# Induced set attention with a leaky feed-forward: the maxima of the first attention by one full-size product, and a shorter pipeline for its first batch

## The chip, the cores and the metric

The kernel runs on one core of a Trainium2 chip. The metric is device time in microseconds (us) from one launch. Engines are named as in the profile: PE is TensorE (matmuls), PEld its weight loads, DVE VectorE, ACT ScalarE, POOL GpSimd, SP the engine that issues most DMAs.

## The reference

Four batches of 12480 tokens with 128 channels pass an induced set attention (32 inducing points), and then a feed-forward with a leaky ReLU.

```python
def mab(q, kv):
    s = scale * (q @ kv.transpose(0, 2, 1))
    s = s - s.max(-1, keepdims=True)
    a = np.exp(s)
    a /= a.sum(-1, keepdims=True) + 1e-09
    return a @ kv
h = mab(I, x)            # first attention: I is [4, 32, 128], x is [4, 12480, 128]
attn = mab(x, h)         # second attention: every token against the 32 rows of h
hid = attn.reshape(49920, 128) @ w_in        # w_in is [128, 2048]
out = np.maximum(0.01 * hid, hid) @ w_out    # w_out is [2048, 128]
```

## The kernel before

A batch is cut into six groups of 2048 tokens and a rest of 192 tokens (`RG`, handled first), so a batch has seven groups. The scores of a group in the first attention stand as a 128 x 512 tile: partition (j, m) holds inducing point m against the j-th quarter of the group's tokens. Softmax over all tokens of a batch needs one maximum per m, kept as a running maximum over the groups. `running(b, g, sp)` (line 273) does this for one group. It is a generator: each `yield` is a place where the caller may put other work. In the kernel before its steps are

- L281, DVE: copy the scores out of PSUM and take each partition's maximum, `rm` [128, 1];
- L292, PE: `mx_ps`, a product of `rm` (as weights, one column) with the 128 x 128 identity. It turns the 128 maxima into one row on one partition;
- L295 and L301, DVE: reduce that row over j to 32 maxima, multiply by -SCALE and repeat four times, `mrow` [1, 128];
- L306, PE: `mb_ps`, a product of `mrow` (as weights, one partition) with a single one. It turns the row back into a column over the 128 partitions;
- L314 or L316, DVE: the running (negated) maximum `nm`;
- L321 and L325, ACT: `al`, the factor for what earlier groups gave, and the exponentials `e` with their sums `zg`; L334, DVE: the running sum `zs`.

Later the exponentials are transposed (L418, `ay`), multiplied with x on PE (`h_ps`, L393, in `accumulate`) and added up on DVE (`hacc`, L408). From the sum comes h (`normalise`: `hs` L458, `hT_ps` L461), which the second attention and the feed-forward of that batch need.

All work is issued in an order written out by hand, and each engine works through its own queue in that order. There are two stages.

The first batch has no other work to hide behind. `first_batch` (line 467) runs rounds: round i transposes group i on PE (`xT_ps`, L501) and copies it on ACT (L504), computes its scores (`s_ps`, L269), and moves earlier groups on by some steps of their generators. Three groups are under way at a time: `accumulate` is called for group i - 3. After each part of a round, steps of background lanes are issued, by the tables `ROUNDS` and `DRAIN`. The lane `l` turns the float64 weights into float32: per quarter of a matrix one ACT operation, six on DVE (L119, L123, L127, L132, L137, L141), two on POOL (L144 and L145), and for w_out a split into high and low parts (ACT L200, POOL L201). The lane `t` transposes w_in (`winT_ps`, L214) and `m` multiplies the weights (`w_ps`, L226, four parts).

After that the feed-forward runs 1568 units, each one product of the first layer (`ph`, L770) and three of the second (`po`, L798), three units ahead: ACT makes `ghi` (L778) and DVE `glo` (L780). Between units, steps of the later batches' first attention (`first_scores`, `first_values`), of the second attention, and of what is left of the weights are issued. 21 of the 28 groups pass `running` here. `yield HEAVY` delays the next steps by three units.

Of the kernel before, what the change touches and what calls it, by code (L numbers as in the profile page):

```python
# [9 lines left out]
F32 = mybir.dt.float32  # L10
# [9 lines left out]
def induced_attention_then_leaky_ffn(  # L20
# [8 lines left out]
    """Induced set attention, then a leaky-relu feed-forward, on 4 x 12480 tokens.  # L29

    The second attention gives x2 = a @ h with a [tokens, 32], so x2 @ w_in = a @ (h @ w_in): the
    first product contracts over 32 only.  Operands are split exactly into float32r parts
    (hi + lo = float32); the four part products of the first product are stacked along the
    contraction, (a_hi, a_hi, a_lo, a_lo) against (W_hi, W_lo, W_hi, W_lo).  With
    g = max(0.01 h, h) = 0.99 relu(h) + 0.01 h, the linear part is a @ (h @ w_in @ w_out).
    The first attention runs over groups of tokens with a running maximum.

    A group holds J tiles of 32 * K tokens: token K * (32 j + r) + k is column (k, r) of tile j,
    so that 32 x 32 transposes lead between [(j, r), (k, m)] and [(j, m), (k, r)].
    """  # L40
    nc = tc.nc
# [23 lines left out]
    # what a long instruction of VectorE weighs in slots of the feed-forward; no lane goes on  # L65
    # before it is paid off
    HEAVY = 3
    # loads of w_in: after which loads of x of the first batch
    LOADS = [3, 4, 7, 10]
    # steps of the lanes (l: weights to float32, t: w_in^T, m: w_in @ w_out, w: h @ w_in) that  # L70
    # run beside the first batch: after each part of a round, of the drain, of the second
    # attention of the first group
    ROUNDS = [[""] * 9, [""] * 4 + ["l"] * 5, *[["l"] * 7 + [""] * 2] * 4, ["l"] * 6 + ["", "l", ""]]
    DRAIN = ["t", "", "l", "l", "", "", "l", "tt", "l", "l", "t", "m", "l", "l"]
# [21 lines left out]
    one = const.tile([1, 1], F32, tag="one", name="one")  # L96
# [10 lines left out]
    def from_double(raw, dst):  # L107
        """float64 words [p, n, (low, high)] to float32 dst [p, n], rounded to nearest.

        The high word, cut to the exponents that float32 has (below them zero, above them  # L110
        infinity), gives sign, exponent and 20 bits of the fraction; the low word the rest.
        """
# [38 lines left out]
    def setup():  # L151
# [9 lines left out]
        nc.vector.memset(one, 1.0)  # L161
# [77 lines left out]
    def load_rows(b, g, q):  # L239
        """x of a group's columns 4 q to 4 q + 3, with tokens (j, r) on the partitions."""  # L240
        _, J, K = GROUPS[g]
        n = min(K, 4)
        t = sb.tile([P, 4, C], F32, tag="xr", name="xr", bufs=XR)
        src = rows_of(b, g).rearrange("(p k) c -> p k c", k=K)
        nc.sync.dma_start(t[: 32 * J, :n, :], src[:, 4 * q : 4 * q + n, :])
        xr[b, g, q] = t

    def load_blocks(b, g, j0, nj):
        """x of tiles j0.., with (block of 32 channels, r) on the partitions."""
# [11 lines left out]
    def columns_product(ps, lhsT, b, g, j):  # L261
        """lhsT^T x^T of tile j, on the partitions (j, m)"""
# [11 lines left out]
    def running(b, g, sp):  # L274
# [4 lines left out]
        if J < 4:  # L279
# [9 lines left out]
        )  # L289
        yield HEAVY  # L290
        pt = aux_ps("mx_ps")
        nc.tensor.matmul(pt[:1, :P], rm, ident, start=True, stop=True)  # L292
        yield
        mrow = sb.tile([1, 5, M], F32, tag="mrow", name="mrow", bufs=2)
        nc.vector.tensor_reduce(  # L295
            out=mrow[:, 4, :],
            in_=pt[:1, :P].rearrange("p (j m) -> p m j", m=M),
            op=ALU.max,
            axis=AX.X,
        )  # L300
        nc.vector.tensor_scalar_mul(  # L301
            mrow[:, :4, :], mrow[:, 4:5, :].broadcast_to([1, 4, M]), -SCALE
        )
        yield
        pb = aux_ps("mb_ps")
        nc.tensor.matmul(  # L306
            pb[:, :1], mrow[:, :4, :].rearrange("p j m -> p (j m)"), one, start=True, stop=True
# [5 lines left out]
        if nm_old is None:  # L313
            nc.vector.tensor_copy(nm, pb[:, :1])  # L314
        else:
            nc.vector.tensor_tensor(out=nm, in0=pb[:, :1], in1=nm_old, op=ALU.min)  # L316
# [23 lines left out]
    def first_scores(b):  # L340
        """exp(scores - running maximum) of each group, with what the earlier ones are to be
        multiplied by, and the sums of the exponentials."""
# [42 lines left out]
    def accumulate(b, g, hacc, al, ay, apart):  # L385
        """hacc * al + the group's exponentials^T x, on the partitions (k % 4, m)"""
# [34 lines left out]
    def first_values(b):  # L421
        """h of a batch: the exponentials against x, then everything that follows from h."""
# [21 lines left out]
    def sums(b):  # L444
        """1 / (the sums of the exponentials + 1e-9), on the partitions (part, m)"""
# [8 lines left out]
    def normalise(b, hacc, rz):  # L454
        """h^T four times side by side, from the sums on the partitions (part, m)"""
# [11 lines left out]
    def first_batch():  # L467
        """h of batch 0, before which there is no other work: rows held on chip, transposed by
        the tensor engine, and exponentials against x as they are."""
# [51 lines left out]
        for i in range(n):  # L521
# [4 lines left out]
            if i >= 2:  # L526
                next(chains[i - 2])
# [431 lines left out]
```

## Time and profile before

| | |
|---|---|
| time, median of 3 runs | 1652.87 us (1651.2 to 1653.23) |
| span of the profiled execution | 1653.0 us |
| TensorE clock granted, mean | 0.994 |
| PE busy | 1627.5 us, 98% of the span |
| DVE busy | 1308.2 us, 79% |
| ACT busy | 1008.5 us, 61% |
| POOL busy | 110.8 us, 7% |

The profiled execution's own time is its span from the first to the last instruction, 1653.0 us, and is within 0.2 us of the median of the timed runs. A matmul's listed duration contains the time it takes to pass through the array, so consecutive matmuls overlap in the list; what one costs the engine is read from start to start. A product of float32 operands (here `mx_ps`, `mb_ps`, `s_ps`, `h_ps`, `z_ps`, `w_ps`) appears as two records each, one of float32r operands (`ph`, `po`) as one.

### The profile page before, as it was taken

What the parts mean: (1) busy time and instruction counts of PE and PEld (TensorE: products, weight loads), DVE (VectorE), ACT (ScalarE), POOL (GpSimd) and SP (SyncE); (2) the same over time, 40 slices, a digit from 0 to 9 for tenths busy, and PEclk for the clock granted to TensorE, in tenths of its full rate; (3) what the DMA queues carried; (4) which work ended last, traced back from release to release, by engine and by line L of the source; (5) the groups of instructions that cost most, each with busy time, mean ns of one, the idle gap of its engine ahead of it and who ended that gap; (6) DMA issues with size and microseconds to landing.
All of it is one profiled execution on the core that took longest, in us unless ns stands there. A gap on an engine that the chain in (4) does not pass through costs nothing.

```text
span 1653.0 us, 22527 instructions
## 1 busy us (share of the span) xinstructions
PE 1627.5 (98%) x7937; PEld 1260.6 (76%) x7937; DVE 1308.2 (79%) x2230; ACT 1008.5 (61%) x1763; POOL 110.8 (7%) x108
## 2 busy tenths in 40 slices
PE   7899999999999999999999999999999999999998
PEld 4577777777777777777777777777777788888886
DVE  6878878778787887777787887888787887777776
ACT  4466656666566665566666656665566666666665
POOL 3310010000001000000000000000010110000000
PEclk9899999999999999999999999999999999999999
DMA  7333234332252333542223233442221112111211
GB/s 258 66 61 52 52 71 76 68 81 63 48 100 48 50 60 78 98 97 48 44 56 74 54 71 70 90 90 58 65 44 39 32 33 44 36 29 39 44 21 19
DMA packets 401504, 104.46 MB, mean 63 GB/s; under 512 B 372432, under 2 KB 374896, under 8 KB 401392
## 3 DMA queue, kind: packets, MB, share of 16 engines
q1 hardware_dynamic: 401344, 103.01, 30.7%
q8 instruction: 63, 1.03, 0.3%
q14 instruction: 49, 0.40, 0.1%
q10 hardware_dynamic: 48, 0.02, 0.0%
HBM read 48.94 MB, written 25.56 MB: 45 GB/s over the span
## 4 chain that ended last, share of the span: by engine, by line
PE 96%; DVE 2%; DMA 0%; ACT 0%; issue 0%; POOL 0%; SPq 0%; POOLq 0%; DVEq 0%
PE po L798 66%; PE ph L770 23%; PE s_ps L269 3%; PE po L804 1%; PE h_ps L393 1%; PE mb_ps L306 0%; DMA xr<-in_x_dram 0%; PE mx_ps L292 0%; DVE cv_b L123 0%; DVE cv_a L137 0%; PE xT_ps L501 0%; DVE ay L418 0%; DVE cv_a L119 0%; PE hw_ps L617 0%; DVE e L281 0%
## 5 line engine op out<-in xcount | busy, mean ns | idle before, releaser
L780 DVE SCALAR_TENSOR_TENSOR glo<-ph,ghi 128x512 fp32r<-128x512 f32 (+1 forms) x1568 | 1053.8, 680 | 318.2 <-ACT ghi L778 311.0
L778 ACT ACTIVATE ghi<-ph 128x512 fp32r<-128x512 f32 (+1 forms) x1568 | 935.0, 597 | 593.8 <-PE ph L770 592.0
L770 PE MATMUL ph<-A,hws 128*128 128x512 f32 (+1 forms) x1600 | 634.4, 400 | 0.9 <-DVE glo L780 0.9
L798 PE MATMUL po<-ghi,w_lo 128*128 128x512 f32 (+1 forms) x1568 | 619.8, 395 | 0.0
L798 PE MATMUL po<-ghi,w_hi 128*128 128x512 f32 (+1 forms) x1568 | 617.4, 394 | 0.0
L798 PE MATMUL po<-glo,w_hi 128*128 128x512 f32 (+1 forms) x1568 | 614.0, 392 | 0.0
L770 PEld LDWEIGHTS ph<-A,hws 128*128 128x128 f32 x1600 | 300.0, 188 | 90.4 <-issue 11.8
L798 PEld LDWEIGHTS po<-glo,w_hi 128*128 128x128 f32 x1568 | 296.1, 189 | 72.0
L798 PEld LDWEIGHTS po<-ghi,w_lo 128*128 128x128 f32 x1568 | 294.6, 188 | 67.8
L798 PEld LDWEIGHTS po<-ghi,w_hi 128*128 128x128 f32 x1568 | 295.3, 188 | 65.8
L712 POOL TENSOR_TENSOR alo<-aT,ahi 128x512 fp32r<-128x512 f32 x24 | 31.1, 1295 | 729.4 <-ACT ahi L707 729.4
L814 DVE STREAM_TRANSPOSE osb<-po 128x512 f32<-128x512 f32 (+1 forms) x98 | 68.9, 703 | 1.7 <-PE po L804 1.7
L667 POOL TENSOR_TENSOR y<-y,mx 128x512 f32<-128x512 f32 (+1 forms) x27 | 25.3, 938 | 446.2 <-DVE mx L665 421.2
L374 DVE STREAM_TRANSPOSE xT<-xc 128x512 f32<-128x512 f32 x72 | 50.4, 701 | 0.0
L681 POOL TENSOR_TENSOR y<-y,sm 128x512 f32<-128x512 f32 (+1 forms) x27 | 25.4, 939 | 206.0 <-DVE sm L679 127.1
L804 PE MATMUL po<-A,m2s 128*128 128x512 f32 (+1 forms) x100 | 38.5, 388 | 0.0
L393 PEld LDWEIGHTS h_ps<-xr,ay 128*32 128x32 f32 (+1 forms) x784 | 24.6, 116 | 12.8 <-issue 12.1
L393 PE MATMUL h_ps<-xr,ay 128*32 128x128 f32 (+1 forms) x784 | 30.6, 290 | 0.0
L269 PE MATMUL s_ps<-xT,indT 128*32 128x512 f32 x192 | 26.9, 622 | 1.4 <-ACT xT L504 1.4
L269 PE MATMUL s_ps<-xT,hT 128*32 128x512 f32 x192 | 25.6, 605 | 0.4 <-ACT hT L463 0.4
L504 ACT COPY xT<-xT_ps 128x512 f32<-128x512 f32 x24 | 13.1, 592 | 18.4 <-PE xT_ps L501 18.3
L306 PEld LDWEIGHTS mb_ps<-one,mrow 1*128 1x128 f32 x56 | 8.6, 191 | 18.3 <-issue 15.4
(99 smaller groups left out, 432.5 us busy)
## 6 DMA issues: line engine op xcount, KB each, us to landing
xr<-in_x_dram SPq DMA_DIRECT2D x96, 256.0 KB, 4.3
out_dram<-osb SPq DMA_DIRECT2D x384, 64.0 KB, 2.2
xc<-in_x_dram SPq DMA_DIRECT2D x288, 64.0 KB, 2.7
A<-ahi SPq DMA_DIRECT2D x190, 64.0 KB, 2.0
A<-alo SPq DMA_DIRECT2D x190, 64.0 KB, 2.0
raw<-in_moe_w_in_dram SPq DMA_DIRECT2D x4, 512.0 KB, 7.6
raw<-in_moe_w_out_dram SPq DMA_DIRECT2D x4, 512.0 KB, 7.3
hws<-hwhi SPq DMA_DIRECT2D x24, 64.0 KB, 2.0
```

Source lines behind the costliest of these rows:

```text
L269: nc.tensor.matmul(dst, lhsT, rhs, start=True, stop=True)
L374: nc.vector.transpose(t[:, j, :], blk.rearrange("p n c -> p (n c)"))
L393: nc.tensor.matmul(hp[32 * k : 32 * k + 32, :C], ay[:rows, 4 * q + k, :], xb[:rows, k, :], start=(q == 0), stop=(4 * q + 4 >= K), tile_pos ...
L667: eng.tensor_tensor(out=yv, in0=yv, in1=mx[:rows, :K].unsqueeze(2).broadcast_to([rows, K, M]), op=ALU.subtract,)
L681: eng.tensor_tensor(out=yv, in0=yv, in1=smv.unsqueeze(2).broadcast_to([rows, K, M]), op=ALU.mult)
L712: (eng or nc.gpsimd).tensor_tensor(out=alo[sl], in0=aT.pop((b, g))[: 32 * J, :], in1=ahi[sl].bitcast(F32), op=ALU.subtract,)
L770: nc.tensor.matmul(ph[:, o : o + w], hw[b][1][:, f * P : (f + 1) * P], A4[t][:, o : o + w], start=True, stop=True,)
L778: nc.scalar.activation(ghi[:, :n], ph[:, :n], AF.Relu)
L780: nc.vector.scalar_tensor_tensor(out=glo[:, :n], in0=ph[:, :n], scalar=0.0, in1=ghi[:, :n].bitcast(F32), op0=ALU.max, op1=ALU.subtract,)
L798: nc.tensor.matmul(po[:, :n], w[:, f, :], r[:, :n], start=(f == 0 and r is ghi and w is w_hi), stop=False)
L804: nc.tensor.matmul(po[:, o : o + w], hw[b][2], a4[:, o : o + w], start=False, stop=(o + w == n),)
L814: nc.vector.transpose(osb[:, :n], po[:, :n])
```

## The change

In `running`, DVE spreads the maxima over four columns instead: `own` [128, 4] is 1 where the column is the partition's own j, so `rd` (L292 of the changed kernel) has -SCALE * rm in column j and zero elsewhere. One PE product of the constant `e128` (128 x 128, which sums over the four partitions that share an m) with `rd` gives every partition the four values of its m. DVE takes the minimum over those four and the old `nm` in one instruction with an accumulator (L308; L305 for a batch's first group). The two products with one row are gone, and the generator has two steps fewer.

In `first_batch`, a group now passes product, minimum and exponentials within the round after its scores, and `accumulate` is called for group i - 2. `ROUNDS` and `DRAIN` are cut to the new numbers of parts.

```diff
-    ROUNDS = [[""] * 9, [""] * 4 + ["l"] * 5, *[["l"] * 7 + [""] * 2] * 4, ["l"] * 6 + ["", "l", ""]]
-    DRAIN = ["t", "", "l", "l", "", "", "l", "tt", "l", "l", "t", "m", "l", "l"]
+    ROUNDS = [[""] * 2, [""] * 4 + ["l"] * 3, *[["l"] * 7 + [""]] * 4, ["l"] * 7 + [""]]
+    DRAIN = ["t", "l", "l", "l", "tt", "l", "t", "lm", "l"]
...
-    one = const.tile([1, 1], F32, tag="one", name="one")
+    own = const.tile([P, 4], F32, tag="own", name="own")
...
-        nc.vector.memset(one, 1.0)
+        nc.vector.tensor_reduce(out=own, in_=ident4, op=ALU.add, axis=AX.X)
...
+        rd = sb.tile([P, 4], F32, tag="rd", name="rd", bufs=2)
+        nc.vector.tensor_scalar(
+            out=rd, in0=own, scalar1=rm, scalar2=-SCALE, op0=ALU.mult, op1=ALU.mult
+        )
         yield HEAVY
-        pt = aux_ps("mx_ps")
-        nc.tensor.matmul(pt[:1, :P], rm, ident, start=True, stop=True)
-        yield
-        mrow = sb.tile([1, 5, M], F32, tag="mrow", name="mrow", bufs=2)
-        nc.vector.tensor_reduce(
-            out=mrow[:, 4, :],
...
-        nc.vector.tensor_scalar_mul(
-            mrow[:, :4, :], mrow[:, 4:5, :].broadcast_to([1, 4, M]), -SCALE
-        )
-        yield
-        pb = aux_ps("mb_ps")
+        pm = aux_ps("mx_ps")
         nc.tensor.matmul(
-            pb[:, :1], mrow[:, :4, :].rearrange("p j m -> p (j m)"), one, start=True, stop=True
+            pm[:, :4], e128.rearrange("p j m -> p (j m)"), rd, start=True, stop=True
         )
         yield
...
-            nc.vector.tensor_copy(nm, pb[:, :1])
+            nc.vector.tensor_reduce(out=nm, in_=pm[:, :4], op=ALU.min, axis=AX.X)
         else:
-            nc.vector.tensor_tensor(out=nm, in0=pb[:, :1], in1=nm_old, op=ALU.min)
+            least = sb.tile([P, 4], F32, tag="least", name="least", bufs=2)
+            nc.vector.tensor_scalar(
+                out=least, in0=pm[:, :4], scalar1=nm_old, scalar2=None,
+                op0=ALU.min, op1=ALU.min, accum_out=nm,
+            )
...
             if i >= 1:
-                next(chains[i - 1])
-                next(chains[i - 1])
-                yield next(bg)
-            if i >= 3:
-                hacc = yield from accumulate(0, order[i - 3], hacc, *ays.pop(i - 3), False)
+                for _ in range(3):
+                    next(chains[i - 1])
                 yield next(bg)
             if i >= 2:
-                drain(chains[i - 2])
-                ays[i - 2] = transposed(0, order[i - 2])
+                hacc = yield from accumulate(0, order[i - 2], hacc, *ays.pop(i - 2), False)
+                yield next(bg)
+            if i >= 1:
+                drain(chains[i - 1])
+                ays[i - 1] = transposed(0, order[i - 1])
                 yield next(bg)
             scores(i)
             yield next(bg)
-            if i >= 1:
-                next(chains[i - 1])
-                next(chains[i - 1])
-                yield next(bg)
...
```

The queue of DVE in one round of the first batch, from the maximum of a group's scores (L281) to the next transpose of exponentials, before:

```order
L281 TENSOR_SCALAR e,rm<-s_ps 128x512
L316 TENSOR_TENSOR nm<-mb_ps,nm 128x1
L119 TENSOR_SCALAR cv_a<-raw 128x512
L123 TENSOR_SCALAR cv_b<-raw 128x512
L127 TENSOR_SCALAR cv_a<-cv_a 128x512
L132 TENSOR_SCALAR cv_a<-cv_a 128x512
L295 TENSOR_REDUCE mrow<-mx_ps 1x32
L301 TENSOR_SCALAR mrow<-mrow 1x128
L137 SCALAR_TENSOR_TENSOR cv_a<-cv_a,cv_b 128x512
L408 SCALAR_TENSOR_TENSOR hacc<-hacc,al,h_ps 128x128
L141 TENSOR_SCALAR cv_b<-cv_a 128x512
L334 SCALAR_TENSOR_TENSOR zs<-zs,al,zg 128x1
```

The same queue, the same place in the changed kernel:

```order
L281 TENSOR_SCALAR e,rm<-s_ps 128x512
L292 TENSOR_SCALAR rd<-own,rm 128x4
L119 TENSOR_SCALAR cv_a<-raw 128x512
L123 TENSOR_SCALAR cv_b<-raw 128x512
L127 TENSOR_SCALAR cv_a<-cv_a 128x512
L132 TENSOR_SCALAR cv_a<-cv_a 128x512
L308 TENSOR_SCALAR least,nm<-mx_ps,nm 128x4
L137 SCALAR_TENSOR_TENSOR cv_a<-cv_a,cv_b 128x512
L403 SCALAR_TENSOR_TENSOR hacc<-hacc,al,h_ps 128x128
L141 TENSOR_SCALAR cv_b<-cv_a 128x512
L329 SCALAR_TENSOR_TENSOR zs<-zs,al,zg 128x1
```

`rd` has come behind the maximum, `least` has taken the place of `mrow`'s two instructions, and from `nm` (now made by `least`) to the sum `zs` of the same group there are three instructions; before, `zs` in this round belonged to the group whose `nm` stands at the top.

The queue of PE in the first units of the feed-forward, around the last parts of the product of the weights (`w_ps`), before:

```order
L798 MATMUL po<-glo,w_hi 128x512
L798 MATMUL po<-ghi,w_lo 128x512
L226 MATMUL w_ps<-wraw,winT 128x128 x4
L770 MATMUL ph<-A_791,hws 128x512
L798 MATMUL po<-ghi,w_hi 128x512
```

And in the changed kernel, where another part of `w_ps` has come here from the time ahead of the feed-forward:

```order
L773 MATMUL po<-ghi,w_lo 128x512
L226 MATMUL w_ps<-wraw,winT 128x128 x4
L745 MATMUL ph<-A_771,hws 128x512
L773 MATMUL po<-ghi,w_hi 128x512
L773 MATMUL po<-glo,w_hi 128x512
L773 MATMUL po<-ghi,w_lo 128x512
L226 MATMUL w_ps<-wraw,winT 128x128 x4
L745 MATMUL ph<-A_771,hws 128x512
```

The last part of `w_ps` stands one unit later than it did, and the third one unit ahead of it, in the feed-forward. The conversion of the last quarter of w_out, which the last part needs, is also one step less far when the feed-forward begins: the first DVE step behind the first units is L132, where it was L137.

## Rows read from the trace of the kernel before

**Rows 1.** Page, part 4: the chain that ended last, share of the span by engine.

```profile
PE 96%; DVE 2%; DMA 0%; ACT 0%; issue 0%; POOL 0%; SPq 0%; POOLq 0%; DVEq 0%
```

**Rows 2.** Weight loads by line, 84 to 1653 us: count | busy, mean ns | idle before.

```profile
L306 PEld LDWEIGHTS mb_ps<-one,mrow 1*128 1x128 f32 x42 | 6.1, 182 | 7.7 <-issue 7.7
...
L292 PEld LDWEIGHTS mx_ps<-ident,rm 128*1 128x1 f32 x42 | 2.0, 81 | 8.2 <-DVE glo L780 4.8 <-issue 3.5
L448 PEld LDWEIGHTS z_ps<-zs,e 128*128 128x128 f32 x6 | 1.1, 188 | 0.3
```

**Rows 3.** Timeline of PE around one `mx_ps`: start us, us, engine, line, instruction.

```profile
99.27 0.40 PE L798 MATMUL po<-ghi,w_lo 128*128 128x512 f32 x1
99.60 0.38 PE L292 MATMUL mx_ps<-ident,rm 128*1 128x128 f32 x2
...
100.25 0.40 PE L798 MATMUL po<-ghi,w_hi 128*128 128x512 f32 x1
```

**Rows 4.** Timeline of PE around one `mb_ps`.

```profile
108.40 0.40 PE L798 MATMUL po<-ghi,w_lo 128*128 128x512 f32 x1
...
108.73 0.38 PE L306 MATMUL mb_ps<-one,mrow 1*128 1x1 f32 x2
...
109.37 0.39 PE L798 MATMUL po<-ghi,w_hi 128*128 128x512 f32 x1
```

**Rows 5.** Timeline of PE around one `z_ps`, weights `e128`.

```profile
417.62 0.39 PE L798 MATMUL po<-glo,w_hi 128*128 128x512 f32 x1
417.85 0.40 PE L798 MATMUL po<-ghi,w_lo 128*128 128x512 f32 x1
418.08 0.28 PE L448 MATMUL z_ps<-zs,e 128*128 128x1 f32 x2
...
418.54 0.40 PE L798 MATMUL po<-ghi,w_hi 128*128 128x512 f32 x1
```

**Rows 6.** Stretches: us, busy of PE, PEld, DVE, ACT, POOL, PEclk, DMA share, GB/s.

```profile
42.00:48.00 6.00, 3.20 (x52) 2.06 (x56) 5.90 (x16) 2.10 (x5) 3.19 (x3) 0.94 0.06 8
48.00:54.00 6.00, 6.00 (x76) 4.96 (x72) 5.15 (x14) 3.52 (x9) 1.54 (x2) 0.50 0.26 40
```

**Rows 7.** DVE by line, 12.1 to 56.6 us: count | busy, mean ns | idle before.

```profile
L301 DVE TENSOR_SCALAR mrow<-mrow 1x128 f32<-1x128 f32 x7 | 3.9, 563 | 0.2
...
L141 DVE TENSOR_SCALAR cv_b<-cv_a 128x512 int32<-128x512 int32 x7 | 2.9, 411 | 0.1
...
L295 DVE TENSOR_REDUCE mrow<-mx_ps 1x32 f32<-1x128 f32 x6 | 1.6, 274 | 0.4 <-PE mx_ps L292 0.4
...
L316 DVE TENSOR_TENSOR nm<-mb_ps,nm 128x1 f32<-128x1 f32 x6 | 0.9, 146 | 0.0
```

**Rows 8.** Timeline: one `mrow` on DVE while POOL works, one while it does not.

```profile
23.88 1.32 POOL L145 TENSOR_TENSOR w_in_sb<-cv_a,cv_t 128x512 f32<-128x512 f32 x1
...
24.32 0.97 DVE L301 TENSOR_SCALAR mrow<-mrow 1x128 f32<-1x128 f32 x1
...
38.30 0.22 DVE L301 TENSOR_SCALAR mrow<-mrow 1x128 f32<-1x128 f32 x1
```

**Rows 9.** Timeline of DVE at the end of the first batch; [idle before <- releaser].

```profile
50.83 0.15 DVE L316 TENSOR_TENSOR nm<-mb_ps,nm 128x1 f32<-128x1 f32 x1
...
52.05 0.22 DVE L334 SCALAR_TENSOR_TENSOR zs<-zs,al,zg 128x1 f32<-128x1 f32 x1
...
54.41 0.35 DVE L408 SCALAR_TENSOR_TENSOR hacc<-hacc,al,h_ps 128x128 f32<-128x128 f32 x1 [0.94 <-PE h_ps L393]
...
56.22 0.35 DVE L408 SCALAR_TENSOR_TENSOR hacc<-hacc,al,h_ps 128x128 f32<-128x128 f32 x1 [0.86 <-PE h_ps L393]
```

**Rows 10.** Timeline at the start of the feed-forward, around the last `w_ps`.

```profile
74.53 0.42 DVE L141 TENSOR_SCALAR cv_b<-cv_a 128x512 int32<-128x512 int32 x1
74.98 1.40 DVE L580 SCALAR_TENSOR_TENSOR hws<-hw_ps,hws 32x512 fp32r<-32x512 f32 x2
...
77.83 1.16 PE L226 MATMUL w_ps<-wraw,winT 128*128 128x128 f32 x8 [0.41 <-POOL wraw L145]
```

More of the change, by code (lines that the diff above doesn't have):

```diff
@@ L289, in running @@
         )
+        rd = sb.tile([P, 4], F32, tag="rd", name="rd", bufs=2)
+        nc.vector.tensor_scalar(
+            out=rd, in0=own, scalar1=rm, scalar2=-SCALE, op0=ALU.mult, op1=ALU.mult
+        )
         yield HEAVY
-        pt = aux_ps("mx_ps")
-        nc.tensor.matmul(pt[:1, :P], rm, ident, start=True, stop=True)
-        yield
-        mrow = sb.tile([1, 5, M], F32, tag="mrow", name="mrow", bufs=2)
-        nc.vector.tensor_reduce(
-            out=mrow[:, 4, :],
-            in_=pt[:1, :P].rearrange("p (j m) -> p m j", m=M),
-            op=ALU.max,
-            axis=AX.X,
-        )
-        nc.vector.tensor_scalar_mul(
-            mrow[:, :4, :], mrow[:, 4:5, :].broadcast_to([1, 4, M]), -SCALE
-        )
-        yield
-        pb = aux_ps("mb_ps")
+        pm = aux_ps("mx_ps")
         nc.tensor.matmul(
-            pb[:, :1], mrow[:, :4, :].rearrange("p j m -> p (j m)"), one, start=True, stop=True
+            pm[:, :4], e128.rearrange("p j m -> p (j m)"), rd, start=True, stop=True
         )
@@ L525, in first_batch @@
                 yield next(bg)
-            if i >= 2:
-                next(chains[i - 2])
             if i >= 1:
-                next(chains[i - 1])
-                next(chains[i - 1])
-                yield next(bg)
-            if i >= 3:
-                hacc = yield from accumulate(0, order[i - 3], hacc, *ays.pop(i - 3), False)
+                for _ in range(3):
+                    next(chains[i - 1])
                 yield next(bg)
             if i >= 2:
-                drain(chains[i - 2])
-                ays[i - 2] = transposed(0, order[i - 2])
+                hacc = yield from accumulate(0, order[i - 2], hacc, *ays.pop(i - 2), False)
[3 more added lines that the diff above has]
+                ays[i - 1] = transposed(0, order[i - 1])
                 yield next(bg)
@@ L540, in first_batch @@
             yield next(bg)
-            if i >= 1:
-                next(chains[i - 1])
-                next(chains[i - 1])
-                yield next(bg)
         bg = iter(DRAIN)
-        next(chains[n - 2])
-        yield next(bg)
-        next(chains[n - 1])
-        yield next(bg)
-        next(chains[n - 1])
-        yield next(bg)
-        hacc = yield from accumulate(0, order[n - 3], hacc, *ays.pop(n - 3), False)
-        yield next(bg)
-        next(chains[n - 1])
-        yield next(bg)
-        next(chains[n - 1])
-        yield next(bg)
-        drain(chains[n - 2])
-        ays[n - 2] = transposed(0, order[n - 2])
-        yield next(bg)
-        next(chains[n - 1])
+        for _ in range(3):
+            next(chains[n - 1])
+            yield next(bg)
+        hacc = yield from accumulate(0, order[n - 2], hacc, *ays.pop(n - 2), False)
         yield next(bg)
@@ L564, in first_batch @@
         ays[n - 1] = transposed(0, order[n - 1])
-        yield next(bg)
-        hacc = yield from accumulate(0, order[n - 2], hacc, *ays.pop(n - 2), False)
         yield next(bg)
```

## The prediction

> **What bounds the kernel now.** I read the chain that ended last first: 96% of it is PE [rows 1], so a part is worth what it takes from PE's queue, and where PE waits, what it takes from the engine it waits for. Hence two stages to price apart. In the feed-forward PE is never without work; there I read PE's timeline from start to start. The weight loads by line show where the small products hurt: 42 loads of `mb_ps` and 42 of `mx_ps` have 7.7 and 8.2 us of idle time ahead of them, six of `z_ps` only 0.3 [rows 2]. The other stage is the first batch, up to about 59 us. The stretches show DVE busy 5.90 of 6.00 us there while PE is busy 3.20, and only at the end, from 48 to 54 us, PE full at a granted clock of 0.50 (1.2 of 2.4 GHz) [rows 6]. So the rounds are DVE's, and their end is shared.
>
> **Feed-forward: two products go, one comes.** Two `po` products follow each other in 0.23 us (417.62 to 417.85 [rows 5]). Around `mx_ps`, the last product ahead of it and the second behind it start 0.98 us apart (99.27 to 100.25 [rows 3]); two steps of 0.23 explain 0.46, so `mx_ps` costs 0.52. The same reading for `mb_ps` gives 0.97 - 0.46 = 0.51 [rows 4]. The idle time of [rows 2], 0.37 to 0.39 us for each of 21 groups, says that all places are alike. The new product is not in the trace. The nearest row is `z_ps`: the same 128 x 128 weights `e128`, float32, one moving column instead of four. It costs 0.69 - 0.46 = 0.23 [rows 5]. From below, it can't be less than nothing, since PE runs it in its own queue; from above I take 0.51, that of the two products with odd shapes. I take 0.23, because what `z_ps` shares with it (the whole array as in `ph` and `po`) is what separates it from them.
>
> 21 groups pass here. At 19, 0.52 + 0.51 - 0.23 = 0.80 us goes: 15.2. At two, by the order of both kernels, the product stands right behind an `s_ps` and shares its idle time, so I count only `mb_ps`: 1.0. Together -16.2 us (-20.6 if the new product were free, -10.9 at 0.51).
>
> A rule of the Trainium skill speaks against this: TensorE: Matmul & The Clock Gate, section LDWEIGHTS (loading the stationary operand), says that a load of P columns takes about P / 1.2 ns, whatever its rows. By it the new loads, 128 columns, would be longer than those of `mx_ps`, one column. The trace agrees on the durations, 188 against 81 ns, but not on what they cost, since it is the longer ones that have no idle time ahead of them.
>
> DVE loses L295, L301 and L316 per group here and gets `rd` and `least`; I cost that at nothing. What hides it is PE's lead of three units, and the maximum is issued three units ahead of its product. Should that cover go, a late `rd` would hold PE's queue, and all `ph` and `po` behind it, by what it is late.
>
> **First batch: DVE's work.** From 12.1 to 56.6 us go seven L301 (3.9), six L295 (1.6) and six L316 (0.9): 6.4 us [rows 7]. The changed order has one conversion step less ahead of `hs`, 0.41 by L141 [rows 7]. Six `rd` come. Like L301 they are SBUF to SBUF and small. L301 takes 0.22 us alone and 0.97 when a POOL operation is under way [rows 8]; its mean is 0.563 [rows 7]. I take the mean, 3.4 (1.3 to 5.8). Six `least` read PSUM; between L316 (0.15) and L295 (0.27) I take 0.25 with the accumulator: 1.5 (0.9 to 1.6). Sum: -6.4 - 0.4 + 3.4 + 1.5 = -1.9 us (-4.6 to +0.6).
>
> On the stretched L301, the Trainium skill (SBUF — State Buffer, section Who interferes with whom) says that a VectorE `tensor_scalar` without an accumulator can lock out GpSimd or be locked out by it for a whole instruction, a reduce or the accumulating form not. By that rule `rd` inherits L301's stretch and `least` has none. Without the lock the six `rd` would be 1.3 and the sum -4.0.
>
> **First batch: its waits.** The pipeline is shorter: `least` makes `nm`, and in the same round `zs` waits for the exponentials made with it. In the trace `zs` starts 1.22 us after `nm` [rows 9]. In the new order two conversion steps and one `hacc` lie between them, some 0.41 + 0.41 + 0.35 = 1.2 us, so I cost the rounds at nothing; behind a waiting `zs` stand the transpose `ay`, the next maximum and `rd`, and PE waits for those. At the end, DVE waits 0.94 + 0.86 us for `h_ps` [rows 9]; one of the three accumulations there now lies in the round before, while the last exponentials have less behind which to hide. I take -1.0 (-1.8 if both waits go, +3.0 if a whole chain of product, `least`, exponentials and `zs` is in the open twice, 1.22 and some 0.3 for the product each time). First batch: -2.9 us (-6.4 to +3.6).
>
> **Start of the feed-forward.** One part of `w_ps` moves from a time in which DVE is waited for into PE's full queue. And the last part waits for the last conversion: it started 77.83 with 0.41 of idle time for POOL's `wraw`, 3.3 us after L141 began [rows 10]. That conversion is now a step further back, with a pair of `hws` operations (1.40 [rows 10]) and a `glo` ahead of L141 which were behind it: some 2.6 us later against one unit (four steps of 0.23, 0.92) by which the product also moves. That is +1.7 us, in which the moved part hides (0 if the conversion is early, +2.6 if nothing absorbs it).
>
> **Sum.** 1653.0 - 16.2 - 2.9 + 1.7 = 1635.6 us against the profiled span, which is 0.1 from the median of the runs shown.
>
> **Rivals.**
> A. The shorter pipeline makes the first batch wait in every round, and that eats the gain. Place: DVE's queue at `zs` and `least`. Price: product and `least` about 0.6, 1.22 to `zs`, and a wait for `h_ps` like 0.94 [rows 9], 2.8 us per round; six rounds 16.8. It would be 1653.0 - 16.2 + 16.8 + 1.7 = 1655.3. It decides from 2.4 us a round on. For it: three groups in flight become two. Against: DVE has nearly no idle time in a round [rows 6], and the conversions that filled it still lie between.
> B. The new product costs PE what the old ones did, 0.51, its two loads of 188 ns in the open: 1653.0 - 10.9 - 2.9 + 1.7 = 1640.9. For it: its loads are longer than those of `mx_ps` [rows 2]. Against: `z_ps`. By the Trainium skill's rule on columns alone (same section as above) it would be near this too.
> C. The first batch gains nothing, because `rd` stretches and waits return: 1653.0 - 16.2 + 1.7 = 1638.5, up to 1642.1 at +3.6. For it: 0.97 in [rows 8], the clock of 0.50 in [rows 6].
> D. `rd` mostly misses POOL, both waits at the end go, and the conversion is not late: 1653.0 - 16.2 - 6.4 = 1630.4.
>
> **How the numbers follow.** Forecast 0.55 (1633 to 1638), C 0.20, D 0.12, B 0.08, A 0.05. The range 1630.5 to 1641.5 holds the forecast, B, nearly all of C and half of D. Faster by over 0.2% (3.3 us, about what a measurement of this kernel can tell from no change) are the forecast, B, C and D; of A a part: 0.95. Within 0.2%: 0.02, slower: 0.03, both from A.
>
> **What would show it.** Right: in the feed-forward one pair `mx_ps` per group, 0.23 us by the reading of [rows 5], no idle time ahead of its loads, and 21 `mb_ps` gone; the first `ph` some 3 us earlier than before; an idle time of about 2 us ahead of the last `w_ps`. Wrong: idle time of 0.3 us or more ahead of the new loads (B); `rd` at 0.9 us on the mean or idle DVE ahead of `zs` in the rounds (C, then A); a clock that falls elsewhere in the first batch. The whole is wrong if PE waits for DVE in the feed-forward.

## The result, and the profile after

The changed kernel took 1636.77 us (median of four runs, 1634.6 to 1637.34) against 1653.05 of the kernel before beside it; the ratio is 0.9898, with an interval of 0.9884 to 0.9912. The forecast was 1635.6. The time is right, but its terms are not: a loss and a gain that the forecast missed have about the same size, and the experiments are mostly about that.

The profiled span went from 1653.0 to 1635.5 us. (The time of that run was 1637.34, 1.8 above its span. So the forecast set its span against the median without an offset that the time holds, and "0.1 from the median" was chance.) The page's parts 1 and 4:

```profile
PE 1605.6 (98%) x7881; PEld 1261.6 (77%) x7881; DVE 1303.2 (80%) x2226; ACT 1008.8 (62%) x1763; POOL 109.7 (7%) x108
...
PE 95%; DVE 3%; ACT 1%; issue 0%; DMA 0%; POOL 0%; SPq 0%; DVEq 0%; POOLq 0%
```

PE lost 21.9 us of busy time and bounds the kernel as before [rows 1]; DVE's share of the chain rose from 2% to 3%.

**The new product.** Weight loads by line, 84 to 1636 us, to be held against [rows 2]:

```profile
L297 PEld LDWEIGHTS mx_ps<-rd,e 128*128 128x128 f32 x42 | 7.7, 188 | 3.4 <-issue 1.7
```

Of the 3.4 us of idle time, 1.7 stand at the two places behind `s_ps`; at the other 19 it is 0.04 us ahead of a load, where `mx_ps` and `mb_ps` had 0.37 [rows 2]. And PE's timeline around one of them (start us, us, engine, line, instruction):

```profile
101.61 0.39 PE L773 MATMUL po<-ghi,w_lo 128*128 128x512 f32 x1
101.84 0.28 PE L297 MATMUL mx_ps<-rd,e 128*128 128x4 f32 x2
101.98 0.48 PE L745 MATMUL ph<-A,hws 128*128 128x512 f32 x1
102.30 0.39 PE L773 MATMUL po<-ghi,w_hi 128*128 128x512 f32 x1
```

The last product ahead and the second behind start 0.69 apart (101.61 to 102.30), as around `z_ps` [rows 5]: 0.69 - 0.46 = 0.23, as forecast. Over all places of the feed-forward (what a place takes beyond the plain pace) 21 `mb_ps` and 19 `mx_ps` made 20.3 us, and the 19 new ones that stand alone make 4.2: -16.1, where -16.2 was forecast.

**The plain feed-forward.** Behind 1425 us nothing stands between the products but one `po<-A,m2s` for each tile of 512 tokens: 16 units of four products and this one, 65 in all. The rows of this product between 1425 and 1580 us (count, duration min/median/max in ns, first and last start) give the pace. Before, and after:

```profile
L804 PE MATMUL po<-A,m2s x10: 395/395/395, 1435.1 to 1571.5; 128*128 128x512 f32 x10
```

```profile
L779 PE MATMUL po<-A,m2s x10: 397/397/398, 1433.5 to 1569.4; 128*128 128x512 f32 x10
```

Nine tiles are 585 products: 136.4 us before, 0.2332 a product, and 135.9 after, 0.2323. The granted clock is 1.00 in both, and neither the instructions nor their order differ there. Over the 6300 products behind the hundredth that would be 5.8 us, if all of them kept this pace; the forecast knew nothing of it.

**The first batch and the start of the feed-forward.** The first `ph` starts at 69.1 us, and before at 68.2: 1 us later, not some 3 earlier. (Seven other traces below have the changed kernel's order up to here; in them it starts at 67.4 to 68.6, and in before_again at 67.4. So that 1 us is within what executions differ by; the 3 us are not there in any of them.) `hT`, which ends the first batch (its copy on ACT), before and after:

```profile
L463 ACT COPY hT<-hT_ps x1: 265/265/265, 58.5 to 58.5; 128x128 f32<-128x128 f32 x1
```

```profile
L458 ACT COPY hT<-hT_ps x1: 267/267/267, 58.3 to 58.3; 128x128 f32<-128x128 f32 x1
```

So the batch gained 0.2 and not 2.9. (In the eight traces `hT` comes at 57.5 to 58.3, and in the traces of the old order at 58.5, at 57.8 in before_again and at 55.3 in before_a4_even, where the granted clock from 48 to 54 us was 0.50, 0.72 and 1.00.) DVE's lines, 12.1 to 56.6 us, show a part of where its saved work went (two rows of before that [rows 7] did not show, then after):

```profile
L123 DVE TENSOR_SCALAR cv_b<-raw 128x512 int32<-128x512 int32 x7 | 5.5, 791 | 0.0
...
L127 DVE TENSOR_SCALAR cv_a<-cv_a 128x512 f32<-128x512 f32 x7 | 3.6, 516 | 0.0
```

```profile
L123 DVE TENSOR_SCALAR cv_b<-raw 128x512 int32<-128x512 int32 x7 | 6.5, 926 | 0.0
L127 DVE TENSOR_SCALAR cv_a<-cv_a 128x512 f32<-128x512 f32 x7 | 5.5, 784 | 0.0
...
L292 DVE TENSOR_SCALAR rd<-own,rm 128x4 f32<-128x4 f32 x6 | 2.5, 416 | 0.2
...
L308 DVE TENSOR_SCALAR_CACHE_REDUCE least<-mx_ps,nm 128x4 f32<-128x4 f32 x6 | 1.3, 216 | 1.2 <-PE mx_ps L297 1.2
L308 DVE DVE_READ_ACCUMULATOR least<-mx_ps,nm 128x1 f32 x6 | 0.5, 81 | 0.0
```

6.4 us went [rows 7], and 2.5 + 1.8 came: -2.1. But two conversion steps, untouched by the change, grew from 9.1 to 12.0. One place of the timelines of POOL and DVE after:

```profile
29.84 1.33 POOL L144 TENSOR_TENSOR cv_t<-cv_t,cv_b 128x512 f32<-128x512 f32 x1 [3.55 <-DVE cv_b L141]
31.25 1.34 POOL L145 TENSOR_TENSOR w_in_sb<-cv_a,cv_t 128x512 f32<-128x512 f32 x1
```

```profile
29.61 0.42 DVE L119 TENSOR_SCALAR cv_a<-raw 128x512 int32<-128x512 int32 x1
29.95 1.51 DVE L123 TENSOR_SCALAR cv_b<-raw 128x512 int32<-128x512 int32 x1
31.38 1.50 DVE L127 TENSOR_SCALAR cv_a<-cv_a 128x512 f32<-128x512 f32 x1
```

An instruction of 0.41 alone takes 1.5 beside an operation of POOL. Before, `mrow` took such a stretch (0.97 [rows 8]); with `mrow` gone the next instruction takes it. The stretch belongs to the pair of DVE's and POOL's operations, and I had booked it as `mrow`'s own time. Over all rows of DVE, from the end of its long first wait to the end of `hs`, what instructions took beyond the shortest of their kind was 12.2 us before and 11.1 after, though `mrow` alone held 2.5 of it.

Still, DVE's work did fall. That stretch took 46.3 us before, 41.8 of work and 4.5 of waits, and 45.4 after, 39.1 of work and 6.3 of waits: work fell by 2.7 (L123 and L127 rose, but L137 fell from 5.5 to 4.8, and `hs`, stretched to 1.37 before, took 0.29), and the waits rose by 1.8. In the second pair, before_again and after_again, it is -2.6 and +3.2. So what DVE's work gave went into waits, with a share that differs between executions. DVE's waits, 12 to 59 us, before and after (total, times, longest; the wait ahead of the first group left out):

```profile
DVE hacc L408 <- PE h_ps L393: 2.1, 3, 0.9
DVE e L281 <- PE s_ps L269: 1.3, 1, 1.3
```

```profile
DVE hacc L403 <- PE h_ps L388: 1.9, 1, 1.9
DVE least L308 <- PE mx_ps L297: 1.2, 2, 0.7
...
DVE rz L445 <- PE z_ps L443: 0.6, 1, 0.6
DVE zs L329 <- ACT e L320: 0.5, 1, 0.5
```

Behind `hT`, stretches of 62 to 68 us (columns as in [rows 6]), before and after:

```profile
62.00:64.00 2.00, 2.00 (x12) 1.27 (x10) 1.91 (x6) 1.11 (x2) 0.00 (x0) 1.00 0.01 2
...
66.00:68.00 2.00, 1.60 (x4) 0.30 (x2) 1.58 (x3) 1.08 (x2) 0.00 (x0) 0.94 0.60 94
```

```profile
62.00:64.00 2.00, 1.36 (x4) 0.29 (x2) 1.91 (x6) 1.12 (x2) 0.00 (x0) 1.00 0.00 0
...
66.00:68.00 2.00, 2.00 (x3) 0.50 (x3) 1.02 (x2) 0.23 (x1) 0.00 (x0) 0.50 0.56 87
```

The part of `w_ps` that moved had kept PE busy at 62 us. Without it PE is busy 1.36 us there, and from 66 to 68 us the granted clock is 0.50 (1.2 of 2.4 GHz) where it was 0.94. That the one follows from the other is not shown: in five of the eight traces of the changed order the clock from 66 to 68 us is 0.67 to 0.92, and the first `ph` comes at 67.4 to 67.7; in the other three it is 0.50, and 68.5 to 69.1. The last `w_ps` waits too, less than the 2 us that the forecast named, but against 0.41 before [rows 10]:

```profile
81.43 1.16 PE L226 MATMUL w_ps<-wraw,winT 128*128 128x128 f32 x8 [1.06 <-POOL wraw L145]
```

Counted from the first `ph`, the hundredth product starts at 98.6 us before and at 100.9 after; from `hT` that is 40.1 and 42.6 us (39.8 to 40.1 in the three traces of the old order, 41.4 to 42.9 in the eight of the new one). And at three places of the feed-forward PE now waits for DVE's `glo`, here 0.24 us (0.47 from start to start in place of 0.23):

```profile
231.47 0.40 PE L773 MATMUL po<-ghi,w_lo 128*128 128x512 f32 x1
231.94 0.50 PE L745 MATMUL ph<-A,hws 128*128 128x512 f32 x1
```

That makes 1.1 us with what follows each. The sum: +2.3 up to the hundredth product, and behind it -16.1, +1.1 and -5.8, which is 1.0 more than -17.5, the difference of the spans. The runs on the pace below put its term at -4.7, and with that the sum is -17.4.

### The profile page after: what moved, and what is told of

Its sections match the earlier page's. It is cut to its first block, busy times and chain, and to the rows that moved or that the text cites. A ratio compares the mean times of both kernels' runs of the same rounds, so it can differ in the third digit from the quotient of the medians.

```text
span 1635.5 us, 22370 instructions
## 1 busy us (share of the span) xinstructions
PE 1605.6 (98%) x7881; PEld 1261.6 (77%) x7881; DVE 1303.2 (80%) x2226; ACT 1008.8 (62%) x1763; POOL 109.7 (7%) x108
## 4 chain that ended last, share of the span: by engine, by line
PE 95%; DVE 3%; ACT 1%; issue 0%; DMA 0%; POOL 0%; SPq 0%; DVEq 0%; POOLq 0%
PE po L773 66%; PE ph L745 23%; PE s_ps L269 3%; PE po L779 1%; PE h_ps L388 1%; DMA xr<-in_x_dram 0%; DVE cv_b L123 0%; PE xT_ps L496 0%; DVE cv_a L127 0%; DVE glo L755 0%; DVE ay L413 0%; ACT ghi L753 0%; PE mx_ps L297 0%; PE winT_ps L214 0%; DVE cv_a L119 0%
## 5 line engine op out<-in xcount | busy, mean ns | idle before, releaser
L745 PE MATMUL ph<-A,hws 128*128 128x512 f32 (+1 forms) x1600 | 627.5, 396 | 1.0 <-DVE glo L755 0.7
L773 PEld LDWEIGHTS po<-ghi,w_lo 128*128 128x128 f32 x1568 | 294.7, 188 | 65.6
L388 PEld LDWEIGHTS h_ps<-xr,ay 128*32 128x32 f32 (+1 forms) x784 | 22.5, 112 | 12.4 <-issue 12.2
L297 PEld LDWEIGHTS mx_ps<-rd,e 128*128 128x128 f32 x56 | 10.5, 202 | 17.4 <-DVE rd L292 14.1
L779 PEld LDWEIGHTS po<-A,m2s 128*128 128x128 f32 x100 | 19.1, 191 | 4.2
```

The costliest lines, as they stand in the source:

```text
L388: nc.tensor.matmul(hp[32 * k : 32 * k + 32, :C], ay[:rows, 4 * q + k, :], xb[:rows, k, :], start=(q == 0), stop=(4 * q + 4 >= K), tile_pos ...
L745: nc.tensor.matmul(ph[:, o : o + w], hw[b][1][:, f * P : (f + 1) * P], A4[t][:, o : o + w], start=True, stop=True,)
L773: nc.tensor.matmul(po[:, :n], w[:, f, :], r[:, :n], start=(f == 0 and r is ghi and w is w_hi), stop=False)
L779: nc.tensor.matmul(po[:, o : o + w], hw[b][2], a4[:, o : o + w], start=False, stop=(o + w == n),)
```

## The experiments

Ratios are to the kernel before, timed on the same chip. The first question was whether the faster pace belongs to the execution or to the kernel, and what each half of the change gives.

**after_again, before_again** (no edit).

> The changed kernel again, to part its gain from the pace of one execution. In the two profiled executions so far the plain feed-forward, at a granted clock of 1.00 in both, took 0.2332 us a product before and 0.2323 after; that is about 5.6 us over the feed-forward. Theory 1 (the pace belongs to the execution, not to the kernel): the gain that the traces explain is 16.1 (products) - 2.4 (first batch and start of the feed-forward) - 1.0 (three waits) = 12.7 us, a ratio of 0.9923, and the ratio of medians drifts from 0.9898 towards it with other pairs of runs. Theory 2 (the pace belongs to the kernel, since fewer odd products leave the later ones undisturbed): ratio 0.990 again, and 0.2323 us a product again.

> The kernel before, for its trace on the same chip as its companions. Theory 1 (pace of the execution): a plain product at 0.2323 to 0.2328 us, a span of 1647 to 1650. Theory 2 (pace of the kernel): 0.2332 us and a span near 1653 again.

After: 1636.19 us, 0.9897 (0.9882 to 0.9912), span 1634.9. Before: span 1652.3. The same row of `po<-A,m2s`, before again and after again:

```profile
L804 PE MATMUL po<-A,m2s x10: 395/395/395, 1434.3 to 1570.8; 128*128 128x512 f32 x10
```

```profile
L779 PE MATMUL po<-A,m2s x10: 397/397/398, 1432.9 to 1568.8; 128*128 128x512 f32 x10
```

136.5 and 135.9 us: theory 1 fell. The pace repeats to a tenth of a microsecond and belongs to the kernel.

**product_alone**: the new product in the old pipeline.

```diff
+            if i >= 2:
+                next(chains[i - 2])
...
-            if i >= 2:
-                hacc = yield from accumulate(0, order[i - 2], hacc, *ays.pop(i - 2), False)
+            if i >= 3:
+                hacc = yield from accumulate(0, order[i - 3], hacc, *ays.pop(i - 3), False)
...
```

> The new product inside the old pipeline over three groups, with the old tables of the first batch. Theory 1 (the gain is all in the products of the feed-forward; the shorter pipeline gave the first batch nothing and the moved part of the product of the weights cost about 2.4): -16.1 in the feed-forward, first ph at 67 to 68.2 us, at most as late as before, and 1 to 3 us faster than the changed kernel: ratio to before 0.988 to 0.990. Rival (the shorter pipeline does gain its 1 us of waits, and without it the first batch is later): 1 us slower than the changed kernel or more, ratio 0.991.

1636.19 us, 0.9898 (0.9884 to 0.9911): no difference from the changed kernel, which neither theory gave. `hT` came at 60.5 us, 2.2 later than with the short pipeline. DVE waited more for the scores (1.3 us in all before):

```profile
L281 DVE TENSOR_SCALAR_CACHE_REDUCE e<-s_ps 128x512 f32<-128x512 f32 x6 | 4.0, 674 | 4.1 <-PE s_ps L269 4.1
```

But this is a single wait, for the second group, whose scores DVE takes up at 14.3 us here and in the changed kernel. From there to `hT` it is 46.3 us against 44.0, with less waiting (3.7 against 5.0) and more work, as stretches make 14.0 us here where they make 11.1 in the changed kernel. From `hT` to the hundredth product it took 40.1 us, as before, and the changed kernel 42.6. So beside the new product the short pipeline gains some 2 us in the first batch, by one trace of product_alone, and its tables, which move a part of `w_ps` into the feed-forward, give 2.5 back.

**pipeline_alone**: the short pipeline with the two old products (five steps of a group in the round after its scores, `DRAIN` the same).

```diff
-                for _ in range(3):
+                for _ in range(5):
                     next(chains[i - 1])
```

> The pipeline over two groups with the two old products. Theory 1: nothing is gained in the feed-forward, and the first batch is as in the changed kernel or later, since a group now passes both one-row products and the two DVE steps between them within a round: +2.4 to +5 us, ratio 1.0015 to 1.003, no idle time of PE beyond 1 us a round. Rival A of the prediction (the short pipeline makes each round wait): +16.8 us, ratio 1.010. Rival (the pipeline itself is what gained): 0.998 or less.

1663.53 us, 1.0067 (1.0054 to 1.0079): slower by more than theory 1 said. `hT` came at 65.6. DVE's waits, 12 to 66 us (total, times, longest; the 7.0 lies ahead of the first group):

```profile
DVE mrow L295 <- PE mx_ps L292: 7.6, 2, 7.0
DVE hacc L408 <- PE h_ps L393: 4.9, 6, 1.4
DVE nm L316 <- PE mb_ps L306: 3.9, 6, 1.0
```

`nm` now waits for `mb_ps` in six rounds and `hacc` for `h_ps` in six. This is rival A's mechanism at about half its price: the way through two products and two DVE steps doesn't fit into one round. The new product's single way does, with the waits shown above, so each half by itself makes the first batch later (by 2 to 2.7 us and by 7 to 8, in one trace each), and both together leave it where it was. Of the other 3 us of pipeline_alone, 2.9 come between `hT` and the hundredth product, where its tables are those of the changed kernel.

Now the pace. `ghi`, `glo` and the weights stand at the same addresses in both kernels. With `mrow` gone, `A4`, the moving operand of `ph`, stands at 206080 bytes of a partition, a multiple of 256, where it had stood at 207232, 128 past one. (An edit that moves `A4` also moves the tiles allocated behind it by as much. Of these PE reads one in the plain stretch, `m2s`, in one product of 65.)

**a4_as_before**: the changed kernel, `A4` back at 207232.

```diff
-        mx = sb.tile([P, 16], F32, tag="mx", name="mx")
+        mx = sb.tile([P, 160], F32, tag="mx", name="mx")
```

> The changed kernel with one tile of the second attention (mx) made 1152 bytes longer in all, so that A4, the moving operand of ph, stands at the address that it has in the kernel before (207232 bytes in each partition in place of 206080); the instructions and their order are the same, and so are the addresses of ghi, glo and of the weights. Theory 1 (the pace of the plain feed-forward hangs on the place of A4, 128 bytes past a multiple of 256 before, a multiple of 256 after): 0.2333 us a product again, +5.7 us, 1642 us, ratio to before 0.9933. Rival (the pace comes from the program, with its odd products gone): 0.2323 as in the changed kernel, 1636 us, ratio 0.990.

```profile
L779 PE MATMUL po<-A,m2s x10: 395/395/395, 1437.3 to 1573.7; 128*128 128x512 f32 x10
```

1641.77 us, 0.9926 (0.9912 to 0.9939), and 136.4 us for nine tiles: theory 1, in the pace and in the time.

**before_a4_even**: the kernel before, `A4` at 206848.

```diff
-        ind = sb.tile([M, C], F32, tag="ind", name="ind", bufs=1)
+        ind = sb.tile([M, C], F32, tag="hs", name="ind", bufs=1)
...
-        mx = sb.tile([P, 16], F32, tag="mx", name="mx")
+        mx = sb.tile([P, 32], F32, tag="mx", name="mx")
```

> The kernel before with mx longer by 128 bytes in all and the tile hs laid on the place of a tile that is used only at the start, so that A4 stands 384 bytes lower (206848), at a multiple of 256 as in the changed kernel; instructions, order and the places of ghi, glo and the weights are those of before. Theory 1 (the place of A4): 0.2323 us a product, -5.7 us, 1647 us, ratio 0.9965. Rival (the program): 0.2333, ratio 1.000.

```profile
L804 PE MATMUL po<-A,m2s x11: 397/397/398, 1427.7 to 1578.7; 128*128 128x512 f32 x11
```

Ten tiles in 151.0 us: 0.2323 a product, the pace of the changed kernel with both old products in the queue. 1647.77 us, 0.9972 (0.9961 to 0.9984). Theory 1 holds in both directions: the pace goes with the place of `A4` and what stands behind it. Behind the hundredth product the two traces differ from their companions, after and before, by +4.8 and -4.7 us, so the term is 4.7 and not all of 5.8. It is not `ph`'s own time either. From start to start, the step behind `ph` went from 234.7 to 233.1 ns, those behind the three `po` from 233.4 to 229.9 (`ghi,w_hi`), from 231.5 to 232.8 (`glo,w_hi`) and from 233.1 to 233.2 (`ghi,w_lo`).

**aligned**: the changed kernel with all operands of `ph` and `po` at multiples of 256.

```diff
-    own = const.tile([P, 4], F32, tag="own", name="own")
+    own = const.tile([P, 64], F32, tag="own", name="own")[:, :4]
...
+    const.tile([P, 32], F32, tag="pad", name="pad")
...
+        sb.tile([P, 40], F32, tag="pad2", name="pad2", bufs=1)
         mx = sb.tile([P, 16], F32, tag="mx", name="mx")
```

> The changed kernel with unused space ahead of the weights, of ghi and glo and of A4, so that all operands of ph and po begin at multiples of 256 bytes (ghi, glo and the weights stand 32 bytes past a multiple of 64 in both kernels so far). Theory 1, if it holds for po as for ph: 3 products of 4 gain as ph does, 3.6 ns each, 0.2296 us a product, -17 us, 1619 us, ratio 0.980. Theory 1 for the moving operand of ph alone, or the rival (the program): 1636 us, ratio 0.990.

```profile
L782 PE MATMUL po<-A,m2s x10: 389/389/389, 1435.0 to 1567.6; 128*128 128x512 f32 x10
```

1605.75 us, 0.9715 (0.9701 to 0.9728): the fastest of all, 30 us under the changed kernel and nearly twice what theory 1 gave. Nine tiles take 132.6 us, 0.2267 a product, each lasting 389 ns. Against after_again that is 35.6 us over 6300 products; 4.9 of it do not come (why stays open), and 1.4 are gained ahead of the hundredth: 32.1, the difference of the spans. In the plain stretch all four steps of a unit are 226.7 ns.

**moving_only**: `ghi`, `glo` and `A4` at multiples of 256, the weights where they were, 32 bytes past a multiple of 64.

```diff
+            if i == XR:
+                sb.tile([P, 24], F32, tag="pad", name="pad", bufs=1)
             t = sb.tile([P, 4, C], F32, tag=kinds[i][0], name="xr0", bufs=kinds[i][1])
...
+        sb.tile([P, 40], F32, tag="pad2", name="pad2", bufs=1)
```

> The changed kernel with unused space ahead of ghi and of A4 alone: ghi, glo and A4, the moving operands of po and ph, begin at multiples of 256 bytes, and all weights (w_hi, w_lo, hws) stay 32 bytes past a multiple of 64, as in the changed kernel. Theory 1 (the moving operand's place sets the pace): 0.2267 us a product as with all aligned, 1605.7 us, ratio 0.9715. Rival (the weights' place does): 0.2323, 1636 us, ratio 0.990. If both count, between.

```profile
L782 PE MATMUL po<-A,m2s x10: 395/395/395, 1438.1 to 1574.6; 128*128 128x512 f32 x10
```

1642.02 us, 0.9935 (0.9922 to 0.9947), 0.2333 a product: slower than both said. Moving operands at 256 gain nothing while the weights stand at 32, and `ghi` and `glo` at their old place (160 past a multiple of 256) were better there.

**moving_64** (pads of 32 and 224 bytes at the same two places).

> As the run with the moving operands alone at multiples of 256 bytes, but ghi and glo at multiples of 64 that are no multiples of 128 (104896); A4 at a multiple of 256. Theory a (only a place that is no multiple of 64 costs much): 1605.7 to 1611 us, ratio 0.9715 to 0.975. Theory b (each place that is no multiple of 256 costs what A4 at 128 cost, 3.7 ns a product, for two of ghi and one of glo in a unit): 0.2267 + 0.0028 = 0.2295 us a product, +17 us, 1623 us, ratio 0.982. Theory c (it must be a multiple of 128 at least, else the whole loss stays): 1636 us.

```profile
L782 PE MATMUL po<-A,m2s x11: 394/396/396, 1428.3 to 1578.9; 128*128 128x512 f32 x11
```

1632.38 us, 0.9877 (0.9864 to 0.989): 150.6 us for ten tiles, 0.2317 a product, near none of the three. So the moving operands' places set no order by themselves: with the weights at 32, `ghi` and `glo` at 160, at 192 and at 0 past a multiple of 256 gave 0.2323, 0.2317 and 0.2333. Of the six sets tried only the one with all at multiples of 256 reaches 0.2267, and against moving_only the weights make that difference. Whether aligned weights alone would do it, and how the place acts, was not tried and stays open.

Two more runs priced the products by themselves.

**narrow_added** and **full_twice**:

```diff
+        if b:
+            nc.tensor.matmul(pm[:1, 8 : 8 + P], rm, ident, start=True, stop=True)
```

```diff
+        if b:
+            nc.tensor.matmul(
+                pm[:, 8:12], e128.rearrange("p j m -> p (j m)"), rd, start=True, stop=True
+            )
```

> The changed kernel with one product more for each of the 21 groups in the feed-forward: the old one of rm (128 x 1, as weights) with the identity, right behind the new product; nothing reads its result. Theory 1 (a product whose weights do not fill the array costs 0.51 in this queue): +0.51 x 21 = +10.7 us, 1647 us, ratio 0.9963, and idle time of about 0.37 us ahead of its weight loads. Rival (a load of one column costs less than one of 128, so a narrow product costs at most what the full one costs, 0.22): +4.7 us or less, 1641 us or less, ratio 0.9927 or less.

> The changed kernel with the new full-size product issued a second time, into other columns of the same PSUM tile, for each of the 21 groups in the feed-forward; nothing reads the second result. Theory 1 (a full-size product of float32 costs 0.225 whatever it is for): +4.7 us, 1641 us, ratio 0.9927, no idle time ahead of its loads. Rival (two such products in a row show the loads of 188 ns in the open, 0.38 more, and the single one hides them behind the product ahead): +8 us or more, 1644 us, ratio 0.995.

PE around one place, with the narrow product and with the full one:

```profile
99.97 0.39 PE L775 MATMUL po<-ghi,w_lo 128*128 128x512 f32 x1
100.20 0.28 PE L297 MATMUL mx_ps<-rd,e 128*128 128x4 f32 x2
100.41 0.38 PE L301 MATMUL mx_ps<-ident,rm 128*1 128x128 f32 x2
...
101.06 0.39 PE L775 MATMUL po<-ghi,w_hi 128*128 128x512 f32 x1
```

```profile
101.00 0.39 PE L777 MATMUL po<-ghi,w_lo 128*128 128x512 f32 x1
101.24 0.28 PE L297 MATMUL mx_ps<-rd,e 128*128 128x4 f32 x2
101.37 0.36 PE L301 MATMUL mx_ps<-rd,e 128*128 128x4 f32 x2
...
101.91 0.39 PE L777 MATMUL po<-ghi,w_hi 128*128 128x512 f32 x1
```

From the `po` ahead to the `po` behind: 1.09 and 0.91 us, and 0.69 without an addition. The narrow product costs 0.40, the second full one 0.22. Times: 1645.42 (0.9953, 0.9939 to 0.9966) and 1641.75 (0.9933, 0.9921 to 0.9946), +9.2 and +5.6 over after_again where 21 times these prices give 8.4 and 4.7. So the dear thing is the product whose weights don't fill the array, not its load: its loads are the short ones (81 against 188 ns). Nor is it that `rm`'s product has 128 moving columns and the new one four. `hT_ps` has 128 x 128 weights and 128 moving columns of float32, and by the same reading costs 0.22 in the feed-forward at all three places (weights x rows, then rows x columns; after):

```profile
L456 PE MATMUL hT_ps<-e,hs x6: 270/272/273, 391.1 to 1129.7; 128*128 128x128 f32 x6
```

The narrow product was 0.40 and not 0.51, and the idle time that I expected ahead of its loads wasn't there (0.4 us in all), so that part of theory 1 was wrong; it stood behind another small product here, and what the missing 0.11 is stays open. The rule of the Trainium skill that the forecast weighed (TensorE: Matmul & The Clock Gate, section LDWEIGHTS (loading the stationary operand)) gives the length of a load by its columns alone. The trace agrees that rows don't count (182 ns for `mb_ps`, one row of 128 columns, 188 for 128 rows) and that one column is shorter (81), but not on the figures: an estimate by the page's P / 1.2 is 107 ns for 128 columns and 1 ns for one. And what a product cost went the other way.

**part_back**: one part of `w_ps` ahead of the feed-forward again, where the clock fell in after and after_again.

```diff
-    RAMP = ["wmwm", "w", "", "ll", "", "w", "", "", "", "w", "wwwl"]
+    RAMP = ["wmw", "w", "", "llm", "", "w", "", "", "", "w", "wwwl"]
```

> The changed kernel with one part of the product of the weights (w_ps) moved back ahead of the feed-forward, behind the second hw_ps, where it stood before. Theory (the granted clock fell to 0.50 at 66 us because PE had no work there, and the part that fills it costs less than what the clock costs): the clock stays above 0.9 from 62 to 68 us, the first ph is at 68.0 to 68.6 (-0.5 to -1.1), and another 0.5 is gained in the feed-forward, which has one part less: 1634.8 us. Rival (the clock falls whatever stands there, as the pause begins earlier): first ph as in the changed kernel or up to 1 us later, at most -0.5 in sum, 1636 us.

The clock stayed at 1.00 from 60 to 72 us and the first `ph` came at 67.5, 1.1 earlier than in after_again, as the theory said. But five traces without this edit have it at 67.4 to 67.7 too, so the 1.1 is not shown to be the moved part's. And the time is 1638.02 (0.9912, 0.9899 to 0.9926), 1.8 slower than after_again. PE's waits in the first units:

```profile
70.04 0.50 PE L745 MATMUL ph<-A,hws 128*128 128x512 f32 x1 [1.62 <-DVE glo L755]
76.29 0.50 PE L745 MATMUL ph<-A,hws 128*128 128x512 f32 x1 [1.34 <-DVE glo L755]
79.33 1.01 PE L226 MATMUL w_ps<-wraw,winT 128*128 128x128 f32 x3 [1.84 <-POOL wraw L145]
```

And what follows from them, a stretch of the same kernel:

```profile
76.00:84.00 8.00, 5.86 (x19) 4.76 (x20) 4.63 (x8) 2.30 (x5) 5.00 (x4) 0.64 0.27 68
```

PE arrives earlier at `glo` and at a conversion that DVE and POOL finish no sooner. It waits 4.8 us, against 1.4 to 2.9 in the eight traces without the edit, and the granted clock is 0.64 in this stretch instead of 1.00 in after. In this run the lost clock was only moved. That the start of the feed-forward is bound by DVE's and POOL's conversions, whichever part PE holds, is argued from it and not shown.

## Why the prediction was right in its time and not in its terms

- **Feed-forward, -16.2**: right in mechanism and size (-16.1, from 0.51, 0.51 and 0.22 a product). Rival B (0.51 for the new product) is refuted by its 0.22 and by full_twice.
- **First batch, -2.9**: the step that failed, by its waits. `hT` moved by -0.2 against the first pair and +0.3 against the second (58.1 against 57.8). DVE's work was forecast at -1.9 and fell by 2.7. "I cost the rounds at nothing" and "I take -1.0" for the end make -1.0; the waits rose by 1.8 (second pair 3.2): the wait for `h_ps` stayed (1.9, in one piece where it had been three), that for `mx_ps` rose from 0.4 to 1.2, and waits for `z_ps` and the exponentials are new. "I take the mean" was no sound price either. `mrow`'s stretch did not go with it: L123 and L127 took 2.9 more. That the work still fell is luck in part, as `hs` met no operation of POOL (0.29 in place of 1.37). Rival C, that this term is nothing "because `rd` stretches and waits return", was the right one here.
- **Start of the feed-forward, +1.7**: from `hT` to the hundredth product +2.5 (+1.3 to +3.1 over all traces). The late conversion held (a wait of 1.06, and 0.73 to 1.84 in the eight traces, against 0.41 to 0.46), but the moved part did not hide in it: its products take 0.8 us of PE's queue of their own. How much a lower clock adds differs from execution to execution.
- **DVE's added work "at nothing"**: three waits for `glo` in the feed-forward, 1.1 us.
- **What was missing**: -4.7 for the place of `A4`. The forecast followed instructions and queues, but removing a tile also moves all that are allocated behind it.

Without that last term the change gives 1641.8 (a4_as_before): rival C's upper end, 6 us above the forecast and just outside its range. The range held because a missed loss and a missed gain met, which is luck. The gain of the change as meant, products and pipeline, is 0.7% (0.9926), of which the pipeline, with its tables, has none (product_alone).

## What to carry to other kernels

Where two engines lock each other out, a stretched duration belongs to the pair: taking one stretched instruction away handed most of the stretch to others here (12.2 us before, 11.1 after), so count an instruction's undisturbed time as the saving. A pipeline with fewer groups under way has to be priced by its waits, one by one, also where the work between them looks long enough. On an engine that is never idle, compare the pace in a stretch where both programs are the same, before the difference is put down to the edit; a tile removed shifts the addresses of others, and here such a shift was over a quarter of the gain. A shorter pipeline is paid for by what a round must hold: with one small product the first batch ended where it had, with two 7 to 8 us later.

## What the runs showed of the hardware

The pace of products with 512 moving columns, at a granted clock of 1.00, hung on where their operands begin within a partition: 0.2333, 0.2332, 0.2323, 0.2317 and 0.2267 us for different sets of places, in a stretch with the same instructions on PE; with all at multiples of 256 bytes it was the shortest, 389 ns listed in place of 391 to 398. The Trainium skill (SBUF — State Buffer, section Operand start alignment) asks for a multiple of the element size only, and says that its rule is about legality, not speed; these runs agree with the first and put a number on the second, 30 us of 1636 in this kernel. The same page (section SBUF: two separate sides) says that on the engines' side only the port pair shared by VectorE and GpSimd causes contention. The stretched 1.5 us of DVE beside POOL agree with it; PE's pace shows that places matter beside that pair, and no run here tells whether PE's own reads or other engines' accesses make the difference.
